# Attention and two MLPs on one core: MLP 2's second product of token blocks 0 and 1 by seven half-size products, in an order set by hand

## The chip, the cores and the metric

The kernel runs on one core of one Trainium2 chip. The metric is the device time of one execution in microseconds (us), taken as the median of several runs; less is better. TensorE (PE) multiplies matrices into PSUM, VectorE (DVE) and ScalarE (ACT) read PSUM and SBUF, GpSimd (POOL) works in SBUF, and SyncE (SP) issues the DMAs.

## The reference

Inputs are float32 (B = 4, H = 8, S = 576, D = 64; 2304 tokens of width 512):

```
kv  = einsum('bhsd,bhse->bhde', k, v)
o   = einsum('bhsd,bhde->bhse', q, kv)
o   = o / sqrt(mean(o*o, -1) + 1e-6) * g_norm
x   = o reshaped to [2304, 512]
x   = relu(x @ w_in)**2 @ w_out                  # MLP 1, hidden width 2048
p   = probs / (probs.sum(-1) + 1e-9)             # [2304, 4]
out = sum over e of p[:, e] * (relu(x @ w1[e]) @ w2[e])   # MLP 2, hidden width 4 x 1024
```

## The kernel before

**Tiling.** The tokens are cut into five blocks: 0 to 3 of 512 tokens, and 4 of 256. The hidden width of each MLP is cut into slices of 256: eight for MLP 1 (v = 0 to 7) and sixteen for MLP 2. MLP 2 goes through its sixteen slices twice: v = 8 to 23 for blocks 0, 1 and 4 (the first group), v = 24 to 39 for blocks 2 and 3 (the second group). Each float32 operand is split into a high part `hi` and a remainder `lo` (`split`, L224: an ACT copy and a POOL subtraction), and a product is three matmuls: lo x hi, hi x lo, hi x hi.

**Units.** The program is a list of units, each a function call that issues the instructions of a small step. f: the first product of one block (24 matmuls per slice, with 512 columns, or 256 for block 4). s: the first product of a pair of blocks, by seven half-size products in Winograd's form (`g1s`, seven units of six matmuls). h: the second product of one block in plain form (`g2b`, L834: six matmuls for 128 tokens, whose result is weighted by p and added into the block's accumulator on DVE, L852). q: the second product of a pair by seven half-size products (`g2q`, L774: fourteen units of three matmuls, output transposed, each added into an accumulator on DVE, L797). Before the change q serves the second group alone; the first group uses h for all its blocks.

**What q needs.** For q the hidden values are already multiplied by p (`hidden_t`, L726, four DVE instructions per slice, from a copy of p spread over the partitions), and the right-hand operands are four quarters b11, b22, b21 and four sums t1 to t4 of the hidden tile `hb` (`second_right`, L741, units r: r0 to r6 split an operand, r7 to r10 form t1 to t4). q's left-hand side needs the weight b and the weight sums bs. For h the hidden tile is split instead by an ACT relu and a DVE instruction (L829, L830).

**Weights.** In the first group each slice's weights are loaded (raw), summed and split (units w: `operands`, `left_sums`, `second_sums`), and the split parts a, a2, b and bs are stored to DRAM; the second group fetches them from there (`fetch`). The sums for a and a2 are made on DVE (tile w), those for bs on POOL (tile ws).

**Order.** `rest()` writes the unit list of MLP 1 and MLP 2, with stretches around the turns set by hand (`TURNS`, `END`). Through the first group the compiler's planner places the instructions on the compute engines and only SP keeps the written order; from v = 25 all engines keep it. At the turn the operands of blocks 2 and 3 are made from their accumulators (units x, `right`); these accumulators stay in SBUF through the first group.

**Buffers.** PSUM has eight banks (pool ps). `tmp` has eight buffers of 2 KB per partition. In the second group `hb` alternates between two tiles.

## Time and profile before

| what | value |
|---|---|
| median of three runs | 1198.81 us (1198.78 to 1198.99) |
| the profiled execution's own time | 1202.84 us |
| its span, from the first to the last instruction | 1201.0 us |
| mean granted TensorE clock | 0.998 |
| busy: PE, DVE, POOL, ACT | 1174.3, 849.4, 709.5, 442.3 us |
| moved by DMA | 186.18 MB |

Busy time is the union of an engine's instructions. PE's matmuls overlap in the record, so that the distance between two starts, not the duration of one, is the price of a matmul. A wait is idle time of an engine ahead of an instruction, with what released it.

### The profile page before, as it was taken

What the parts mean: (1) busy time and instruction counts of PE and PEld (TensorE: products, weight loads), DVE (VectorE), ACT (ScalarE), POOL (GpSimd) and SP (SyncE); (2) the same over time, 40 slices, a digit from 0 to 9 for tenths busy, and PEclk for the clock granted to TensorE, in tenths of its full rate; (3) what the DMA queues carried; (4) which work ended last, traced back from release to release, by engine and by line L of the source; (5) the groups of instructions that cost most, each with busy time, mean ns of one, the idle gap of its engine ahead of it and who ended that gap; (6) DMA issues with size and microseconds to landing.
All of it is one profiled execution on the core that took longest, in us unless ns stands there. A gap on an engine that the chain in (4) does not pass through costs nothing.

```text
span 1201.0 us, 15349 instructions
## 1 busy us (share of the span) xinstructions
PE 1174.3 (98%) x5642; PEld 982.7 (82%) x5642; DVE 849.4 (71%) x1268; ACT 442.3 (37%) x825; POOL 709.5 (59%) x588
## 2 busy tenths in 40 slices
...
GB/s 294 236 68 36 71 18 35 53 19 71 40 43 62 36 141 93 233 217 181 221 213 175 191 232 191 200 226 274 166 288 133 222 191 260 158 256 190 205 193 70
DMA packets 49392, 186.18 MB, mean 155 GB/s; under 512 B 5122, under 2 KB 13314, under 8 KB 37030
## 3 DMA queue, kind: packets, MB, share of 16 engines
...
q8 instruction: 45, 0.74, 0.2%
...
q10 hardware_dynamic: 288, 0.04, 0.0%
...
## 4 chain that ended last, share of the span: by engine, by line
PE 87%; DVE 5%; POOL 4%; issue 2%; ACT 1%; DMA 0%; POOLq 0%; DVEq 0%; ACTq 0%
PE p L842 18%; PE p L554 14%; PE p L540 13%; PE pc L679 8%; PE pa L679 8%; PE pd L679 8%; PE pb L679 4%; PE qc L784 3%; PE qd L784 3%; PE qa L784 3%; PE qb L784 2%; POOL hl L226 1%; PE pk L443 1%; PE po L458 1%; DVE u L261 1%
## 5 line engine op out<-in xcount | busy, mean ns | idle before, releaser
L842 PE MATMUL p<-b,hh 128*128 128x512 f32 x640 | 207.8, 390 | 0.5 <-ACT hh L829 0.5
L554 PE MATMUL p<-hh,b 128*128 128x512 f32 (+1 forms) x640 | 191.1, 371 | 0.0
L226 POOL TENSOR_TENSOR hl<-r,hh 128x512 fp32r<-128x512 f32 (+1 forms) x80 | 104.7, 1316 | 77.6 <-ACT hh L225 73.6
L540 PE MATMUL p<-x,a 128*128 128x512 f32 (+1 forms) x720 | 148.8, 362 | 0.2 <-POOL x L226 0.2
L842 PEld LDWEIGHTS p<-b,hh 128*128 128x128 f32 x640 | 120.3, 188 | 25.1 <-ACT hh L829 0.7
L540 PEld LDWEIGHTS p<-x,a 128*128 128x128 f32 x720 | 122.8, 189 | 22.1 <-POOL x L226 0.7
L554 PEld LDWEIGHTS p<-hh,b 128*128 128x128 f32 x640 | 117.6, 189 | 20.7 <-ACT hh L225 0.3
L561 DVE TENSOR_TENSOR acc<-p,acc 128x512 f32<-128x512 f32 (+1 forms) x140 | 86.1, 631 | 61.1 <-PE p L554 60.7
L852 DVE SCALAR_TENSOR_TENSOR acc<-p,p_sb,acc 128x512 f32<-128x512 f32 x150 | 108.8, 745 | 26.1 <-PE p L842 26.0
L842 PE MATMUL p<-b,hl 128*128 128x512 f32 x320 | 125.0, 391 | 0.2 <-DVE hl L830 0.2
L554 PE MATMUL p<-hl,b 128*128 128x512 f32 (+1 forms) x320 | 118.9, 372 | 3.4 <-POOL hl L226 3.4
L679 PE MATMUL pd<-o,a 128*128 128x512 f32 x384 | 98.0, 390 | 1.2 <-DVE pb L699 1.2
L679 PE MATMUL pa<-o,a 128*128 128x512 f32 x384 | 97.8, 390 | 0.0
L679 PE MATMUL pc<-o,a 128*128 128x512 f32 x384 | 97.7, 390 | 0.0
L679 PEld LDWEIGHTS pd<-o,a 128*128 128x128 f32 x384 | 71.9, 188 | 17.1 <-DVE pb L699 2.3
L226 POOL TENSOR_TENSOR a<-w,a 128x512 fp32r<-128x512 f32 x42 | 55.8, 1345 | 50.1 <-ACT a L225 50.1
L679 PEld LDWEIGHTS pc<-o,a 128*128 128x128 f32 x384 | 71.9, 188 | 15.4 <-DVE u L694 0.6
L679 PEld LDWEIGHTS pa<-o,a 128*128 128x128 f32 x384 | 72.0, 188 | 15.2 <-ACT p L690 0.3
L226 POOL TENSOR_TENSOR a<-raw,a 128x512 fp32r<-128x512 f32 x32 | 42.7, 1334 | 56.2 <-ACT a L225 56.2
L226 POOL TENSOR_TENSOR b<-raw,b 128x512 fp32r<-128x512 f32 x32 | 40.7, 1293 | 56.5 <-ACT b L225 56.5
L554 PEld LDWEIGHTS p<-hl,b 128*128 128x128 f32 x320 | 60.6, 189 | 15.5 <-POOL hl L226 5.6
L842 PEld LDWEIGHTS p<-b,hl 128*128 128x128 f32 x320 | 60.2, 188 | 11.8 <-DVE hl L830 0.5
(183 smaller groups left out, 2353.1 us busy)
## 6 DMA issues: line engine op xcount, KB each, us to landing
raw<-in_w SPq DMA_DIRECT2D x65, 512.0 KB, 4.2
a_kept<-a SPq DMA_DIRECT2D x32, 1024.0 KB, 8.5
a<-a_kept SPq DMA_DIRECT2D x32, 1024.0 KB, 10.4
b_kept<-b SPq DMA_DIRECT2D x16, 1024.0 KB, 6.7
bs_kept<-o SPq DMA_DIRECT2D x16, 1024.0 KB, 9.7
bs<-bs_kept SPq DMA_DIRECT2D x16, 1024.0 KB, 7.6
...
kvm<-in_kvm SPq DMA_DIRECT2D x10, 512.0 KB, 3.7
```

The costliest lines, as they stand in the source:

```text
L226: nc.gpsimd.tensor_tensor(out=lo, in0=full, in1=hi.bitcast(F32), op=ALU.subtract)
L261: nc.vector.scalar_tensor_tensor(out=u.bitcast(F32), in0=k, scalar=1.125 * 2.0**-15, in1=u.bitcast(F32), op0=ALU.is_ge, op1=ALU.mult,)
L443: nc.tensor.matmul(pk[:, :P], m[:, 0, n, :], m[:, 1, n, :], start=(n == 0), stop=False)
L458: nc.tensor.matmul(po[done : done + n, c * P : (c + 1) * P], q[:, c, done : done + n], kvd[(b * NPAIR + c) % NKVD], start=True, stop=True,)
L540: nc.tensor.matmul(pt[:, :n], w, x, start=(i == 0), stop=(i == len(steps) - 1))
L554: nc.tensor.matmul(pt[:, :n], w, h, start=(i == 0), stop=(i == len(steps) - 1))
L561: nc.vector.tensor_tensor(out=a, in0=pt[:, :n], in1=a, op=ALU.add)
L679: nc.tensor.matmul(pr[bank], x, y, start=(m == 0 and not more), stop=(m == len(steps) - 1), skip_group_check=more,)
L784: nc.tensor.matmul(pt, x, y, start=(m == 0 and not more), stop=(m == len(steps) - 1), skip_group_check=more)
L842: nc.tensor.matmul(pt, h, w, start=(i == 0), stop=(i == len(steps) - 1))
L852: nc.vector.scalar_tensor_tensor(out=a, in0=pt, scalar=pe, in1=a, op0=ALU.mult, op1=ALU.add)
```

## The change

In the first group the second product of blocks 0 and 1 is made by q units too; block 4 keeps h. So the transposed output holds blocks 0 to 3, and the first group's slices get the whole machinery of q: hidden values weighted by p, seven operand splits and four sums per slice. The sums t3 and t4 go to DVE in both groups. The splits of b and bs (`split_dma`) become two ACT copies (hi, and minus hi) and an accumulating DMA from POOL's queue that adds the full value. To make room, blocks 2 and 3 are stored to DRAM at the start of MLP 2 (units d10 and d11) and read back at the turn (d12 to d14); `hb` becomes a single tile in the space of block 2; p's spread copy is loaded anew every four slices (unit E, which is d7); tiles move between pools, and `tmp` has seven buffers. The loads, stores and weight steps become units of their own (d: `move`, u: `prepare`), and from x0.11 on all engines keep the written order: `FIRST` for v = 8, `STEPS` for v = 9 to 21, `TURN` for 22 to 24, `LATER` for 25 to 38 and `END`. In these lists S is the next s unit, q the next q unit of the slice before, p, v, n the previous, this and the next slice. The end of MLP 1 has a new order as well (`CHANGE`, not shown), in which x0 is cut into twelve units, with the sums of block pairs made in place.

```diff
-N2 = 2 * 512
-T2 = BLK[2][0] // P
+N2 = 4 * 512
+T4 = N2 // P
...
-    if v < NS1:
-        return [f"g{v}.{j}.{c}" for j in blk[::-1] for c in range(KD)]
-    if v >= V2:
-        return [f"q{v}.{n}" for n in (*range(6), 7, 6, *range(8, 14))]
-    return [f"h{v}.{j}.{t}" for j in blk[::-1] for t in range(BLK[j][1] // P)]
+    return [f"g{v}.{j}.{c}" for j in blk[::-1] for c in range(KD)]
...
+FIRST = """
+x0.11 s8.0.0 d8.7 d8.10 u8.7 s8.0.1 u8.8 s8.0.2 r8.0 s8.0.3 d9.0 u9.0 s8.0.4 s8.0.5 u8.9 r8.9 d8.5 u9.1 r8.5
+r8.7 r8.8 f8.4.0 d8.11 s8.0.6 d9.2 d9.7 d8.4 d8.6 r8.3 f8.4.1
+""".split()
+
+STEPS = """
+S q u{v}.3 q S r{p}.1 r{p}.4 h{p}.4.0 u{v}.5 r{p}.10 u{v}.4 S r{p}.2 q S u{v}.2 d{v}.4 q r{p}.6 d{n}.0 q
+u{v}.7 h{p}.4.1 q q S u{v}.8 d{n}.2 r{v}.0 S q q r{v}.9 r{v}.7 q S q u{v}.9 r{v}.3 q E q d{v}.6 u{n}.0 u{n}.1
+r{v}.5 f{v}.4.0 d{v}.5 q f{v}.4.1 r{v}.8
+""".split()
+
+TURN = """
+s22.0.0 q21.0 u22.3 r21.2 q21.1 h21.4.0 r21.1 r21.4 u22.4 q21.2 s22.0.1 s22.0.2 u22.5 r21.10 u22.2 s22.0.3
...
+LATER = """
+S d{v}.9 r{p}.1 d{n}.8 r{p}.4 r{p}.10 q r{p}.2 q S q S S q q r{p}.6 q S q q q r{v}.0 r{v}.7 q q r{v}.3 S q q
+r{v}.9 S q r{v}.8 r{v}.5
+""".split()
+
...
 END = """
...
+r38.4 s39.2.0 r38.10 q38.0 q38.7 q38.1 s39.2.1 s39.2.2 d39.9 s39.2.3 q38.10 q38.2 q38.8 s39.2.4 r38.2 r38.1
+r39.0 s39.2.5 r39.7 r38.6 r39.8 q38.6 s39.2.6 r39.4 r39.10 r39.9 q38.9 q38.12 q38.5 q38.4 q38.3 q39.0 r39.3
+q38.13 r39.5 q38.11 q39.7 r39.1 q39.2 r39.2 r39.6 q39.9 q39.1 q39.3 q39.8 q39.10 q39.5 q39.11 q39.12 q39.6
+q39.4 q39.13
+""".split()
...
+def second_stage():
+    r = list(FIRST)
+    for v in range(NS1 + 1, NV - 1):
+        if v == V2 - 2:
+            r += TURN
+        if V2 - 2 <= v <= V2:
+            continue
+        i, q = 0, iter([f"q{v - 1}.{n}" for n in (*range(6), 7, 6, *range(8, 14))])
+        for u in STEPS if v < V2 else LATER:
+            if u == "S":
+                r.append(f"s{v}.{GRP2[v >= V2][0][0]}.{i}")
+                i += 1
+            elif u == "q":
+                r.append(next(q))
+            elif u == "E":
+                r += [f"d{v + 1}.7"] * ((v + 1 - NS1) % (F2 // FS) == 0)
+            else:
+                r.append(u.format(v=v, p=v - 1, n=v + 1))
+    return r + END
...
-    tmp = ctx.enter_context(tc.tile_pool(name="tmp", bufs=8))
+    tmp = ctx.enter_context(tc.tile_pool(name="tmp", bufs=7))
...
-    def split(hi, lo, full):
+    def split(hi, lo, full, engine=nc.gpsimd):
         nc.scalar.activation(out=hi, in_=full, func=AF.Copy)
-        nc.gpsimd.tensor_tensor(out=lo, in0=full, in1=hi.bitcast(F32), op=ALU.subtract)
+        engine.tensor_tensor(out=lo, in0=full, in1=hi.bitcast(F32), op=ALU.subtract)
+
+    def split_dma(hi, lo, full):
+        nc.scalar.activation(out=hi, in_=full, func=AF.Copy)
+        nc.scalar.activation(out=lo, in_=hi.bitcast(F32), func=AF.Copy, scale=-1.0)
+        nc.gpsimd.dma_start(out=lo.bitcast(F32), in_=full, accum_op=ALU.add)
...
+    def bs_tile(v):
+        if v % 2:
+            return ext.tile([P, 2, 2, 512], F32R, tag="b3", name=f"bs{v}")
+        if v >= V2:
+            return xp.tile([P, 2, 2, 512], F32R, tag="xt", name=f"bs{v}", bufs=1)
+        return spare[0]
+
+    def keep(v, tag, t):
+        w_kept[v, tag] = kept.tile(list(t.shape), F32, name=f"{tag}_kept{v}")
+        nc.sync.dma_start(out=w_kept[v, tag], in_=t.bitcast(F32))
+
+    def move(v, n):
+        s = slice_of(v) - NS1
+        if n in (0, 2):
+            raw[v, n] = rawp.tile([P, 2, HW], F32, tag="raw", name=f"raw{v}_{n}")
+            nc.sync.dma_start(out=raw[v, n], in_=w32[s, :, n : n + 2, :])
...
+        elif n == 4:
+            keep(v, "a", w_t[v][0])
+            keep(v, "a2", w_t[v][1])
+        elif n == 5:
+            keep(v, "b", w_t[v][2])
+        elif n == 6:
+            keep(v, "bs", w_t[v][3])
+        elif n == 7:
+            load_p(v)
...
+            bs = bs_tile(v)
+            w_t[v] += [b, bs]
...
+        elif n in (10, 11):
+            j = n - 8
+            x_kept[j] = kept.tile([P, KD, 512], F32, name=f"x_kept{j}")
+            nc.sync.dma_start(out=x_kept[j], in_=acc_t[j])
+        elif n == 12:
+            t = xp.tile([P, KD, 512], F32, tag="xt", name="xk3", bufs=1)
+            nc.sync.dma_start(out=t, in_=x_kept[3])
+            acc_t[3] = [t[:, :2], t[:, 2:]]
+        else:
+            t = rawp.tile([P, 2, HW], F32, tag="raw", name=f"xk2_{n}")
+            nc.sync.dma_start(out=t, in_=x_kept[2][:, (n - 13) * 2 : (n - 12) * 2, :])
+            acc_t[2] = [t, None] if n == 13 else [acc_t[2][0], t]
+
+    def prepare(v, n):
+        if n == 0:
+            r = raw[v, 0].rearrange("p c (k f) -> p (c k) f", k=2)
+            w_t[v] = [wp.tile([P, 2, KD, FS], F32R, tag=tag, name=f"{tag}{v}") for tag in ("a", "a2")]
+            w_full[v] = left_full(v, r[:, 0:2], r[:, 2:4])
+        elif n in (1, 2):
+            r = raw[v, 0].rearrange("p c (k f) -> p (c k) f", k=2)
+            a = w_t[v][n - 1].rearrange("p x k (h f) -> p x (k h) f", h=2)
+            split(a[:, 0, 0:4, :], a[:, 1, 0:4, :], r[:, :, (n - 1) * P : n * P])
+        elif n in (3, 4):
+            left_split(v, n - 3, w_full[v][n - 3])
+        elif n == 5:
+            b = wp.tile([P, 2, FC, DM], F32R, tag="b", name=f"b{v}")
+            w_t[v].append(b)
+            split_dma(b[:, 0], b[:, 1], raw[v, 2])
+        elif n in (7, 8):
+            r = raw[v, 2]
+            if n == 7:
+                w_sums[v] = ext.tile([P, 2, HW], F32, tag="ws", name=f"ws{v}")
+            t = w_sums[v]
+            a11, a21, a12, a22 = (r[:, f, h * FS : (h + 1) * FS] for f in range(2) for h in range(2))
+            s2, s3, s4, s1 = (t[:, f, h * FS : (h + 1) * FS] for f in range(2) for h in range(2))
+            if n == 7:
+                nc.gpsimd.tensor_tensor(out=s1, in0=a21, in1=a22, op=ALU.add)
+                nc.gpsimd.tensor_tensor(out=s3, in0=a11, in1=a21, op=ALU.subtract)
+                return
+            nc.gpsimd.tensor_tensor(out=s2, in0=s1, in1=a11, op=ALU.subtract)
+            nc.gpsimd.tensor_tensor(out=s4, in0=a12, in1=s2, op=ALU.subtract)
+        else:
+            bs = bs_tile(v)
+            w_t[v].append(bs)
+            split_dma(bs[:, 0], bs[:, 1], w_sums.pop(v))
+
+    w_full, w_sums, x_kept = {}, {}, {}
...
+    def load_p(v, e=None):
+        t0 = pair_of(v)[0] * 4
+        if e is None:
+            e = (slice_of(v) - NS1) * FS // F2
+            if v == NS1:
+                t = p_t[v] = ext.tile([P, 2, 2, 512], F32, tag="a3", name="pb8")[:, 0]
+            elif v == V2:
+                t = p_t[v] = hp.tile([P, 2, 512], F32, tag="hl", name=f"pb{v}")
+            else:
+                if "u" not in p_t:
+                    p_t["u"] = accp.tile([P, 2, 2, 512], F32, tag="acc3", name="pu")
+                t = p_t["u"][:, 0]
+        else:
+            t = spare[0][:, e % 2].bitcast(F32)
...
+        if i == 7:
+            nc.vector.tensor_tensor(out=b11, in0=b12, in1=b11, op=ALU.subtract)
+        elif i == 8:
+            t2 = t_tmp["x"] = [tmp.tile([P, 512], F32, tag="tmp", name=f"t2_{g}_{k}") for k in range(2)]
+            for k in range(2):
+                nc.vector.tensor_tensor(out=t2[k], in0=b22[:, k], in1=b11[:, k], op=ALU.subtract)
+        elif i == 9:
+            nc.vector.tensor_tensor(out=b12, in0=b22, in1=b12, op=ALU.subtract)
+        elif i == 10:
+            t2 = t_tmp.pop("x")
+            for k in range(2):
+                nc.vector.tensor_tensor(out=b21[:, k], in0=b21[:, k], in1=t2[k], op=ALU.subtract)
...
+        if not full_t:
+            full_t.append(accp.tile([P, 4, 512], F32, tag="acc2", name="hb"))
+        pb = p_t[v] if v in p_t else p_t["u"][:, 0] if v < V2 else spare[0][:, e % 2].bitcast(F32)
...
-            engine = nc.vector if v in (V2, NV - 1) else nc.gpsimd
+            engine = nc.vector if v in (NS1, V2, NV - 1) or name in SUMS else nc.gpsimd
...
+    SUMS = ("t3", "t4")
...
-        adds = {"p6": (c12, c21), "p7": (c22,)}.get(p, ())
-        for c in adds:
-            nc.gpsimd.tensor_tensor(out=c, in0=c, in1=u2, op=ALU.add)
-        if p == "p7":
+        adds = {"p6": (c12, c21), "p7": (c22,)} if g else {"p6": (c22, c12, c21)}
+        for c in adds.get(p, ()):
+            engine = nc.gpsimd if g or c is not c22 else nc.vector
+            engine.tensor_tensor(out=c, in0=c, in1=u2, op=ALU.add)
...
-        if v >= V2:
+        if v >= NS1 and j in pair_of(v):
...
-    m = order.index("s25.2.0")
-    with tc.manual_schedule(engines={nc.sync.engine}):
-        for name in order[n:m]:
-            run(name)
     with tc.manual_schedule():
-        for name in order[m:]:
+        for name in second_stage():
```

## Rows read from the trace of the kernel before

**Rows 1.** The page's first part: busy us, share of the span, instructions.

```profile
PE 1174.3 (98%) x5642; PEld 982.7 (82%) x5642; DVE 849.4 (71%) x1268; ACT 442.3 (37%) x825; POOL 709.5 (59%) x588
```

**Rows 2.** Busy us of PE, PEld, DVE, ACT, POOL by stretch; clock, DMA share, GB/s.

```profile
40.00:240.00 200.00, 193.73 (x1007) 163.03 (x1006) 144.35 (x216) 103.27 (x194) 114.35 (x86) 0.99 0.20 64
...
464.00:490.00 26.00, 24.83 (x118) 20.07 (x117) 19.80 (x32) 10.81 (x21) 22.90 (x21) 1.00 0.52 206
...
567.41:593.45 26.04, 26.04 (x127) 22.02 (x126) 15.90 (x26) 8.14 (x15) 13.16 (x14) 1.00 0.56 203
...
912.00:1175.00 263.00, 263.00 (x1162) 217.86 (x1161) 206.76 (x315) 64.41 (x113) 191.96 (x152) 1.00 0.57 206
1175.00:1201.00 26.00, 16.57 (x65) 11.08 (x63) 17.74 (x28) 3.57 (x6) 15.95 (x12) 0.95 0.22 81
```

**Rows 3.** PE's waits, 463 to 890 us: total, times, longest.

```profile
PE p L842 <- ACT hh L829: 0.5, 1, 0.5
PE pd L679 <- DVE pb L699: 0.4, 1, 0.4
PE p L842 <- DVE hl L830: 0.2, 1, 0.2
```

**Rows 4.** PE in order of time: start, us, instructions; one slice.

```profile
567.41 1.52 PE L679 MATMUL pa<-o,a 128*128 128x512 f32 x6
568.77 1.52 PE L679 MATMUL pb<-o,a 128*128 128x512 f32 x6
...
579.65 1.60 PE L540 MATMUL p<-xb,a 128*128 128x256 f32 x12
581.09 0.40 PE L842 MATMUL p<-b,hh 128*128 128x512 f32 x1
...
593.45 1.52 PE L679 MATMUL pa<-o,a 128*128 128x512 f32 x6
```

**Rows 5.** DVE groups, whole run: count, busy us, mean ns, idle before.

```profile
L852 DVE SCALAR_TENSOR_TENSOR acc<-p,p_sb,acc 128x512 f32<-128x512 f32 x150 | 108.8, 745 | 26.1 <-PE p L842 26.0
...
L797 DVE TENSOR_TENSOR acct<-qa,acct 128x512 f32<-128x512 f32 x60 | 41.3, 688 | 12.1 <-PE qa L784 12.1
...
L830 DVE SCALAR_TENSOR_TENSOR hl<-p,hh 128x256 fp32r<-128x256 f32 x32 | 13.5, 422 | 10.8 <-ACT hh L829 10.8
```

**Rows 6.** Tile w, the weight sums on DVE: min/median/max ns.

```profile
L399 DVE TENSOR_TENSOR w<-raw x16: 415/426/1128, 435.6 to 796.2; 128x256 f32<-128x256 f32 x16
...
L400 DVE TENSOR_TENSOR w<-w,raw x16: 412/877/958, 436.3 to 797.5; 128x256 f32<-128x256 f32 x16
```

**Rows 7.** POOL and ACT groups, whole run.

```profile
L226 POOL TENSOR_TENSOR b<-hb,b 128x512 fp32r<-128x512 f32 x32 | 41.3, 1292 | 10.2 <-ACT b L225 10.2
...
L225 ACT ACTIVATE b<-hb 128x512 fp32r<-128x512 f32 x32 | 19.8, 620 | 2.5 <-DVE hb L736 2.5
```

**Rows 8.** Tile ws, the second weight sums on POOL.

```profile
L329 POOL TENSOR_TENSOR ws<-raw x16: 732/738/972, 470.8 to 821.9; 128x256 f32<-128x256 f32 x16
```

**Rows 9.** SP's queue in order of time, the same slice.

```profile
583.51 0.43 SPq L284 DMA_DIRECT2D b_kept<-b  x1
```

**Rows 10.** The list of DMA issues: count, KB each, median us to landing.

```profile
raw<-in_w SPq DMA_DIRECT2D x65, 512.0 KB, 4.2
a_kept<-a SPq DMA_DIRECT2D x32, 1024.0 KB, 8.5
a<-a_kept SPq DMA_DIRECT2D x32, 1024.0 KB, 10.4
...
o<-p_kept SPq DMA_DIRECT2D x4, 512.0 KB, 7.4
```

**Rows 11.** DVE groups at the turn, 853.8 to 882 us.

```profile
L616 DVE TENSOR_TENSOR t<-acc,t 128x512 f32<-128x512 f32 x4 | 5.8, 1446 | 0.0
L607 DVE TENSOR_TENSOR o<-t,o 128x512 fp32r<-128x512 f32 x4 | 4.3, 1087 | 0.2 <-ACT o L605 0.2
```

More of the change, by code (lines that the diff above doesn't have):

```diff
@@ L273, in split_w @@
         if len(parts) == 2:
-            left_sums(parts[0][0], *(full for _, full in parts))
+            for n, full in enumerate(left_full(parts[0][0], *(full for _, full in parts))):
+                left_split(parts[0][0], n, full)
             parts.clear()
@@ L402, in left_sums, with left_split @@
         nc.vector.tensor_tensor(out=s4, in0=a12, in1=s2, op=ALU.subtract)
-        for n in range(2):
-            a = w_t[v][n].rearrange("p x k (h f) -> p x (k h) f", h=2)
-            split(a[:, 0, 4:8, :], a[:, 1, 4:8, :], st[n].rearrange("p m k f -> p (m k) f"))
+        return [t.rearrange("p m k f -> p (m k) f") for t in st]
+    def left_split(v, n, full):
+        a = w_t[v][n].rearrange("p x k (h f) -> p x (k h) f", h=2)
+        split(a[:, 0, 4:8, :], a[:, 1, 4:8, :], full)
     def left(v, tile, x, op, k):
@@ L514, in fused_kernel @@
     h_t, acc_t = {}, {}
-    n_h = [0]
     def new_h(v, j):
-        pool, more = (ext, "3") if ext is not None and n_h[0] % 3 == 2 else (hp, "")
-        n_h[0] += 1
-        h_t[v, j] = [
-            pool.tile([P, FC, 512], F32R, tag=t + more, name=f"{t}{v}_{j}") for t in ("hh", "hl")
-        ]
+        h_t[v, j] = [hp.tile([P, FC, 512], F32R, tag=t, name=f"{t}{v}_{j}") for t in ("hh", "hl")]
         return h_t[v, j]
@@ L529, in g1 @@
         if fc == 0:
-            new_h(s, j)
+            if s < NS1:
+                new_h(s, j)
+            else:
+                pool, tag = (ext, "ws") if s == V2 - 1 else (hp, "hl")
+                t = pool.tile([P, 2, FC, n], F32R, tag=tag, name=f"h{s}_{j}")
+                h_t[s, j] = [t[:, 0], t[:, 1]]
         pt = ps.tile([P, 512], F32, tag="ps", name=f"p1_{s}_{j}_{fc}")
@@ L590, in right @@
             return
-        o = xp.tile([P, 2, 4, 512], F32R, tag="xs", name=f"o{g}_{i}", bufs=4)
-        if len(OPS[i]) == 1:
+        (b11, b21), (b12, b22) = (
+            acc_t[j] if isinstance(acc_t[j], list) else (acc_t[j][:, :2], acc_t[j][:, 2:]) for j in pair
+        )
+        if i == 7:
[10 more added lines that the diff above has]
+                nc.vector.tensor_tensor(out=b21[:, k], in0=b21[:, k], in1=t2[k], op=ALU.subtract)
@@ L593, in right @@
+        if i > 6:
+            return
+        n, m = divmod(i, 2)
+        name = OPS[n][m]
+        if m == 0:
+            o_new[n] = xp.tile([P, 2, 4, 512], F32R, tag="xs", name=f"o{g}_{n}", bufs=4)
+        o = o_new[n]
+        if name == "t4":
             spare[0] = o[:, :, 2:4, :]
             if g:
-                load_p(0)
-                load_p(1)
-        for m, name in enumerate(OPS[i]):
-            o_t[pair[0], name] = (o, m * 2)
-            for k in range(2):
-                hi, lo = o[:, 0, m * 2 + k, :], o[:, 1, m * 2 + k, :]
-                if name[0] == "b":
-                    split(hi, lo, x_part(pair, name, k))
-                    continue
-                full = t_sum(pair, name, k)
-                nc.scalar.activation(out=hi, in_=full, func=AF.Copy)
-                engine = nc.gpsimd if k else nc.vector
-                engine.tensor_tensor(out=lo, in0=full, in1=hi.bitcast(F32), op=ALU.subtract)
@@ L609, in t_sum @@
[L609 to L632 removed]
+                load_p(V2, 0)
@@ L636, in right_first @@
+                load_p(V2, 1)
+        o_t[pair[0], name] = (o, m * 2)
+        engine = nc.gpsimd if name in ON_POOL else nc.vector
+        hi, lo = (o[:, x, m * 2 : m * 2 + 2, :] for x in range(2))
+        if name == "t2":
+            for k in range(2):
+                split(hi[:, k], lo[:, k], t_tmp["x"][k], engine)
+        else:
+            split(hi, lo, dict(b11=b11, t1=b11, b21=b21, t4=b21, b22=b22, t3=b12)[name], engine)
+    o_new = {}
     def right_first(i):
```

273 lines of the change are left out of this document (84 added, 189 removed).

## The prediction

> **What bounds the kernel now.** I began with busy time by engine [rows 1]: TensorE (PE) is busy 98% of the span, every other engine 71% or less. A busy share can hide slow or idle matmuls, so I next cut the span into stages [rows 2]. In one slice of MLP 2's first group (567.41 to 593.45) PE is busy for all 26.04 us, at a granted clock of 1.00 (the 2.4 GHz level), while VectorE (DVE) has 15.9 us of work, GpSimd (POOL) 13.2 and the DMA engines a share of 0.56. PE's waits over that whole group come to 1.1 us [rows 3], so its length is its matmuls. In the second group (912 to 1175) PE is never idle either; DVE has 206.8 of 263 us and POOL 192.0.
>
> The price of a matmul is read from the start times in PE's timeline [rows 4], not from durations, since matmuls overlap. Six with 512 columns take 568.77 - 567.41 = 1.36 us, 0.2267 us each; twelve with 256 columns take 581.09 - 579.65 = 1.44 us, 0.12 each. A slice holds 42 (seven products) + 48 (h of blocks 0 and 1) + 12 (h of block 4) = 102 of the first kind and 24 of the second: 23.12 + 2.88 = 26.0 us, the slice seen [rows 4]. The model closes, so matmuls can be priced by count.
>
> **What the change removes from PE.** Per slice the 48 matmuls of the pair's second product become 14 units of 3 = 42. Six fewer are 1.36 us, a slice becomes 24.64 us, and 16 slices save **21.8 us**. The second group's matmuls are as before. This holds while everything else keeps under PE.
>
> **DVE per slice.** One second-group slice is 84 matmuls = 19.04 us of PE, so its window holds 13.8 slices and DVE has 206.8 / 13.8 = 15.0 us in each [rows 2]: 14 additions of q, 5 of the first product, 4 masked products. A slice of the first group now has these, plus t3 and t4 (2 x 0.69, by the addition of the same width [rows 5]), the four weight sums (3 x 0.43 + 0.88, by their medians [rows 6]), block 4's two hidden pieces and two accumulations (2 x 0.42 + 2 x 0.745) [rows 5]: 20.9 of 24.64 us, 85%. In the second group t3 and t4 move to DVE: 16.4 of 19.04, 86%. Full, but below PE.
>
> **POOL and ACT per slice.** POOL: seven operand splits, two sums (t1, t2), four splits of a and a2, 13 x 1.29 [rows 7], and four weight sums of 0.74 [rows 8]: 19.7 of 24.64 us, 80%. In the second group it falls by two sums, to 60%. The splits of b and bs leave POOL for two ACT copies and a DMA issued on POOL's queue that adds the full value in SBUF. ACT copies of 512 elements take 0.62 [rows 7]; with four of double width at up to 1.24 it has about 13 us, no limit. POOL's cost of issuing such a transfer is not in this trace: it lies between nothing and the 2.5 us each that would fill POOL's 5 us of slack. The operation nearest in kind is a store's issue on SP, 0.43 us [rows 9]; I take that, and the slack covers it.
>
> **The accumulating transfer** has no row either. It moves 512 KB and also reads its destination. From below it is a 512 KB load, 4.2 us; from above, by bytes moved, a 1 MB store, 8.5 us [rows 10]. b is not needed until the next slice, many us later. bs is the tight one: u9 stands after 7 first-product units (S), 2 h and 11 q of its step, which is 9.5 + 2.7 + 7.5 = 19.7 us; its first reader is the second q of the next step, at 24.64 + 1.36 + 0.68 = 26.7. That leaves 7 us behind PE's place in the order, and about 9.5 if ACT and POOL run a little ahead, as they can: bs's sums stand at 14.3 us, and only t1 (its hidden half ready near 16, done by 17.3) is ahead on POOL. I take the upper bound of 8.5 as just covered: cost 0. Behind it on SP is the store of bs, which PE does not wait for.
>
> **Single buffers and SP's order.** hb is one tile now where two alternated, so a hidden write waits for the splits of the slice before. The tightest is b22: its split r1 stands at 4.1 us of the step, the new write follows the sixth S at 15.6, 11 us behind; b21 has 12. POOL at 80% lags by less, so 0; a POOL later than that would hold DVE's queue, with the q additions in it, and then PE. On SP every d unit waits at the head of the queue: the stores of a and a2 (behind split u2) stand ahead of the next slice's load d0, placed at 10.2 us and wanted by u0 at 21.1; it lands in 4.2 [rows 10], so 6 us are left, and 0. DMA share: 0.56 of 26.04 us is 14.6 us for 5 MB, so 2 x 0.5 MB more, counted once or twice, make 17.5 to 20.4 of 24.64, at most 83%.
>
> **The start.** The hidden tile hb now lives in acc2, which holds MLP 1's block 2 until its 1 MB copy to DRAM (d8.10) has landed. Block 2's last g is followed only by g7.4 (24 x 0.12 = 2.9 us) and then s8.0.0 and s8.0.1 (2.7 us) before DVE wants to write hb. A store takes up to 8.5 us [rows 10]: DVE then stands 3 us late, and the additions queued behind it release the bank that the fifth product accumulates in. Against that, 1.2 us of idle at this place before [rows 2] may vanish. Bounds -1 and +4; I take **+1.5**.
>
> **New reloads of the probabilities** (E: slices 12, 16, 20). Each may go only after the seventh product's hidden write (about 20.4 us into the step), takes 7.4 us [rows 10], and is wanted at 28.7: just in time, from 0 to about 2 us each. I take **+0.5** in all.
>
> **The turn** (slices 22, 23, 24; PE 24.64 + 24.64 + 19.04 = 68.3 us). DVE has 3 x 15.0, eight t sums (5.5), one set of weight sums (2.2), block 4 (1.7 + 4.5), two closing additions (1.4), and x1's differences and lo parts. At the old turn four of eight differences took 1.446 us and the lo parts 1.087 [rows 11], against about 0.69; eight differences are then 8.5 us and six lo parts 6.5. Sum 75 us: 7 more than PE has. The surplus can be put off in part into the slices behind, each with 2.6 us of slack. Bounds 0 and 7; I take **+4**. POOL's 25 operand steps, 7 weight splits, 8 weight sums, 4 double splits of x1 and 4 closing additions are 63 us, 92%.
>
> The Trainium skill, page "SBUF — State Buffer" (section Who interferes with whom), says that a DVE instruction with two SBUF inputs contends with a GpSimd instruction that reads SBUF. This trace agrees where both are loaded: the 1.446 us differences [rows 11] and the 0.88 us weight sum beside one of 0.43 [rows 6]. Applied to every such instruction, the rule makes rival 1, below, 1187 to 1195; with the mix of these rows the sum is mine.
>
> **The end, and the rest.** In the last 26 us PE is busy for 16.6 [rows 2], and two chains of three closing additions on POOL (3 x 1.29 us each [rows 7]) stand in it. The new END brings all p5, p6 and p7 ahead of the last products, so the last chain goes earlier: between 0 and 3.9, I take **-1**. The tmp pool falls from 8 buffers to 7; that can only hurt where MLP 1 and the attention live on it. PE's idle time there is 6.3 us in 40 to 240 [rows 2], so I bound it by doubling, 0 to +6, and take 0, a choice: nothing in these rows names a tmp buffer as what PE waits for. The spills and reloads of blocks 2 and 3 (4 MB) have no reader for many us, beyond the start and the turn.
>
> **Sum.** -21.8 + 1.5 + 0.5 + 4 - 1 = -16.8 us. The profiled execution ran 1202.84 us with a span of 1201.0; its changed span should be 1184. The median of the runs is 1198.81, 4 us below that execution, so the forecast is **1182.0 us**.
>
> **Rivals.**
> 1. *DVE becomes the bound* at the turn and in part elsewhere. If every DVE instruction with two SBUF inputs ran at the worst seen (t3 and t4 1.446, weight sums 0.96 [rows 6, 11]), a first-group slice would need 24.1 of 24.64, a second-group one 17.9 of 19.04, and the turn up to 8 us more. For it: POOL rises from 50% to 80%, so it is met more often. Against it: DVE still has 2 to 15% over in steady slices. Late queues would cost some 5 to 12 us more: 1187 to 1195.
> 2. *The accumulating transfer lands late.* It is one wait per slice: PE's second q waits for bs. Every us beyond the 9.5 costs 1 us x 15 slices; from 10.6 us on, the 16.8 is gone, and at 12 us the kernel takes 1182 + 37 = 1219. For it: the a and a2 stores (2 MB) travel in the same stretch, and 1 MB reloads take 10.4 [rows 10]. Against it: twice the bytes of a 4.2 us load are 8.5.
> 3. *Nothing lost*: start, turn and reloads hidden, end shorter: 1198.8 - 21.8 - 2 = 1175.
> 4. *POOL's issue is dear* (above 2.5 us each): POOL passes 24.64 and sets the slice; each 0.5 us more costs 1.0 per slice and 16 in all, so at 3 us each the kernel ends near 1198.
>
> The Trainium skill, page "DMA: Bandwidth & Descriptors" (section Anatomy of one DMA), fits a GpSimd-issued transfer as 2.0 us + bytes / 436 GB/s, an estimate of 3.2 us for 512 KB; by it rival 2 would not happen and the sum stays as it is. No row of this trace shows such a transfer.
>
> **How the numbers follow.** My forecast (1176 to 1187) has 0.63, rival 1 0.18, rival 3 0.05, rival 2 0.10, rival 4 0.04. About 0.2% (2.4 us) is what a measurement here can tell from no change. Faster: 0.63 + 0.18 + 0.05 = 0.86; slower: 0.10 + 0.01; same: 0.03. The range takes my forecast's cases, rival 1 and the terms' lower bounds: 1175 to 1195.
>
> **What would show it.** PE start to start 24.6 us per slice in the first group, with PE waits under 0.3 us each; the second group's slices unchanged at 19.04; a PE wait on DVE near the first hidden writes (hb behind the store of block 2) and one of some us between slices 22 and 24; DVE 83 to 88% and POOL 78 to 90% in steady slices; the accumulating transfers landing within 9 us. A regular PE wait for bs at the second q of every step, or POOL above 97%, would make it wrong.

## The result, and the profile after

The changed kernel runs in 1187.36 us (median of four, 1185.91 to 1189.08), the kernel before in 1198.9 beside it: a ratio of 0.9898 [0.9878, 0.9917]. That is 11.5 us less, not the 16.8 of the sum. The profiled execution took 1188.53 us with a span of 1186.7, against 1202.84 and 1201.0. One of the runs below (after_tail) had a profile in a slowed execution, so of that kernel only times are told.

The page's first part, which answers to [rows 1]: PE is still busy for nearly the whole span; DVE and POOL have come up.

```profile
PE 1152.6 (97%) x5546; PEld 965.7 (81%) x5546; DVE 947.5 (80%) x1414; ACT 498.7 (42%) x871; POOL 795.9 (67%) x662
```

Busy time by stretch (columns as in [rows 2]): a steady slice of the first group, the turn, the second group.

```profile
560.00:585.00 25.00, 25.00 (x123) 21.18 (x122) 21.23 (x35) 11.56 (x18) 21.27 (x21) 1.00 0.81 258
850.00:875.00 25.00, 20.06 (x82) 14.71 (x81) 24.06 (x33) 8.59 (x13) 21.46 (x15) 1.00 0.93 326
900.00:1160.00 260.00, 259.89 (x1147) 214.87 (x1146) 221.10 (x341) 61.85 (x109) 156.26 (x123) 1.00 0.57 207
```

PE in order of time in the steady part, the same unit (block 4's h) in two successive slices:

```profile
560.68 1.52 PE L885 MATMUL p<-b,h 128*128 128x512 f32 x6
...
585.35 1.52 PE L885 MATMUL p<-b,h 128*128 128x512 f32 x6
```

585.35 - 560.68 = 24.67 us for a slice, forecast 24.64. In that stretch PE is busy for 25.00 of 25 us, DVE for 21.23 (85%, forecast 85%), POOL for 21.27 (85%; the sum had 80%, and its own list of signs 78 to 90%); the DMA share is 0.81 (bound 0.83). Between 480 and 845 us PE has no wait in the list. In the second group PE is busy for 259.89 of 260, DVE 85%, POOL 60%. The steady state came out as worked out; the loss lies at the seams, which are the start of slice 8, the turn and the end.

PE's waits from 463 to 890 us, where [rows 3] had 1.1 us:

```profile
PE pa L711 <- DMA a<-a_kept: 3.0, 1, 3.0
PE qb L830 <- ACT t L233: 2.1, 1, 2.1
PE pa L711 <- ACT p L722: 1.7, 2, 1.0
PE qb L830 <- POOL t L234: 1.1, 1, 1.1
PE pd L711 <- DVE pb L731: 0.9, 1, 0.9
PE pc L711 <- DVE u L726: 0.8, 1, 0.8
PE pa L711 <- POOL o L234: 0.4, 1, 0.4
PE qd L830 <- POOL t4b L234: 0.3, 1, 0.3
```

Of these 10.3 us, 2.4 stand in slice 8 (0.69 of the waits for p, and those for pc and pd), 7.9 at the turn, between 851 and 881 us. The 1.1 us of [rows 3] are slice 8's alone; the old turn had one wait, shown first, and the two longest of the new one follow:

```profile
896.33 0.74 PE L784 MATMUL qc<-t,bs 128*128 128x512 f32 x2 [1.12 <-POOL t L226]
```

```profile
860.03 0.49 PE L830 MATMUL qb<-t,bs 128*128 128x512 f32 x1 [2.13 <-ACT t L233]
878.22 1.66 PE L711 MATMUL pa<-o,a 128*128 128x512 f32 x6 [2.98 <-DMA a<-a_kept]
```

The whole turn, from slice 22's first matmul to slice 25's first (columns as above):

```profile
801.91:878.22 76.31, 68.39 (x316) 55.19 (x314) 69.97 (x99) 30.84 (x45) 65.06 (x51) 1.00 0.83 280
```

PE has the 68.4 us of matmuls that were forecast (68.3) and 7.9 of waits. DVE is busy for 70.0 us of the 76.3, where the prediction's sum had 75, and POOL for 65.1 (forecast 63).

The turn in detail, POOL, then ACT, then DVE in order of time; the bracket is the idle time ahead of a group and what ended it:

```profile
851.06 2.37 POOL L234 TENSOR_TENSOR o<-xk,o 128x1024 fp32r<-128x1024 f32 x1 [0.84 <-ACT o L233]
...
854.65 1.74 POOL L234 TENSOR_TENSOR t<-t3f,t 128x512 fp32r<-128x512 f32 x1
856.34 1.75 POOL L234 TENSOR_TENSOR b<-hb,b 128x512 fp32r<-128x512 f32 x1
858.04 1.27 POOL L786 TENSOR_TENSOR t2f<-hb,t1f 128x512 f32<-128x512 f32 x1
860.05 1.47 POOL L234 TENSOR_TENSOR t<-t2f,t 128x512 fp32r<-128x512 f32 x1 [0.74 <-ACT t L233]
```

```profile
849.90 1.06 ACT L233 ACTIVATE o<-xk 128x1024 fp32r<-128x1024 f32 x1 [1.23 <-DMA xk<-x_kept]
...
859.34 0.63 ACT L233 ACTIVATE t<-t2f 128x512 fp32r<-128x512 f32 x1 [5.39 <-POOL t2f L786]
```

```profile
853.61 3.33 DVE L644 TENSOR_TENSOR xk<-xk,t 128x512 f32<-128x512 f32 x2
```

PE's product qb at 860.03 needs t2, and t2 is the last of POOL's row: an operand of x1 at double width (2.37), three splits, then the sum t2f, done at 859.31; ACT, idle for 5.39 us, copies it and POOL splits it. Two of POOL's splits take 1.74 and 1.75 us instead of 1.28 while DVE makes x1's in-place differences (3.33 for two). SP's queue in the same stretch:

```profile
864.54 3.23 SPq L844 DMA_DIRECT2D out<-acct  x3
867.86 2.19 SPq L319 DMA_DIRECT2D a<-a_kept  x2
```

The fetch of a for slice 25 stands behind three output stores. They hold SP's queue for 3.23 us, most of it waiting for the results that they store (each issue takes 0.33 to 0.96 us), and PE meets the fetch late by 2.98 us.

The end, POOL, DVE and then SP's queue:

```profile
1171.54 1.30 POOL L851 TENSOR_TENSOR acct<-acct,acct 128x512 f32<-128x512 f32 x1
1172.80 2.53 POOL L851 TENSOR_TENSOR acct_r<-acct_r,acct 128x512 f32<-128x512 f32 x2
1175.27 1.27 POOL L851 TENSOR_TENSOR acct<-acct,acct 128x512 f32<-128x512 f32 x1
1176.49 2.49 POOL L851 TENSOR_TENSOR acct_r<-acct_r,acct 128x512 f32<-128x512 f32 x2
```

```profile
1176.57 0.69 DVE L838 TENSOR_TENSOR acct<-qc,acct 128x512 f32<-128x512 f32 x1 [2.40 <-POOL acct L851]
```

```profile
1175.35 4.00 SPq L844 DMA_DIRECT2D out<-acct_r  x2
1179.44 1.37 SPq L844 DMA_DIRECT2D out<-acct  x3
```

PE's last group:

```profile
1174.06 0.84 PE L830 MATMUL qd<-t4b,b 128*128 128x512 f32 x3
```

It ends at 1174.06 + 0.84 = 1174.90, 11.8 us before the span's end; before, it ended at 1194.57 with 6.4 us behind it. POOL goes from splits straight into six closing additions, 1171.54 to 1178.98, and DVE stands 2.40 us for one of them. SP's queue waits too: its second store, of POOL's last sum, can go only at 1179.01, and the other six of the eight stand behind it, the last issued at 1182.19. Of the 5.4 us more behind PE, some 2.7 are the later last addition (4.1 us behind PE's end, before 1.4) and some 2 the seven stores left to issue after it, where before there were four.

### The profile page after: what moved, and what is told of

Its sections match the earlier page's. It is cut to its first block, busy times and chain, and to the rows that moved or that the text cites. A ratio compares the mean times of both kernels' runs of the same rounds, so it can differ in the third digit from the quotient of the medians.

```text
span 1186.7 us, 15541 instructions
## 1 busy us (share of the span) xinstructions
PE 1152.6 (97%) x5546; PEld 965.7 (81%) x5546; DVE 947.5 (80%) x1414; ACT 498.7 (42%) x871; POOL 795.9 (67%) x662
## 4 chain that ended last, share of the span: by engine, by line
PE 86%; DVE 5%; DMA 3%; POOL 2%; issue 2%; ACT 1%; SPq 0%; POOLq 0%; DVEq 0%; ACTq 0%
PE p L578 15%; PE p L564 13%; PE pa L711 8%; PE pc L711 8%; PE pd L711 8%; PE qc L830 7%; PE qa L830 7%; PE qd L830 7%; PE pb L711 4%; PE qb L830 3%; PE p L885 3%; PE po L483 1%; PE pk L468 1%; DMA b_kept<-b 1%; DMA a<-a_kept 1%
## 5 line engine op out<-in xcount | busy, mean ns | idle before, releaser
L234 POOL TENSOR_TENSOR b<-hb,b 128x512 fp32r<-128x512 f32 x64 | 85.1, 1331 | 71.7 <-ACT b L233 68.5
L233 ACT ACTIVATE b<-hb 128x512 fp32r<-128x512 f32 x64 | 40.1, 628 | 168.8 <-PE qa L830 162.8
L234 POOL TENSOR_TENSOR a<-w,a 128x512 fp32r<-128x512 f32 x42 | 59.9, 1428 | 73.0 <-ACT a L233 73.0
L711 PEld LDWEIGHTS pd<-o,a 128*128 128x128 f32 x384 | 71.9, 188 | 16.5 <-DVE pb L731 1.6
L838 DVE TENSOR_TENSOR acct<-qc,acct 128x512 f32<-128x512 f32 x90 | 61.7, 686 | 4.3 <-POOL acct L851 4.3
L838 DVE TENSOR_TENSOR acct<-qa,acct 128x512 f32<-128x512 f32 x90 | 61.4, 684 | 0.1
L234 POOL TENSOR_TENSOR t<-t3f,t 128x512 fp32r<-128x512 f32 x32 | 43.4, 1356 | 21.3 <-ACT t L233 21.3
L830 PE MATMUL qd<-t4b,b 128*128 128x512 f32 x192 | 54.5, 391 | 0.6 <-POOL t4b L234 0.3
L830 PE MATMUL qa<-b,b 128*128 128x512 f32 x192 | 53.8, 389 | 0.0
```

The lines of the kernel that those rows point to most:

```text
L233: nc.scalar.activation(out=hi, in_=full, func=AF.Copy)
L234: engine.tensor_tensor(out=lo, in0=full, in1=hi.bitcast(F32), op=ALU.subtract)
L711: nc.tensor.matmul(pr[bank], x, y, start=(m == 0 and not more), stop=(m == len(steps) - 1), skip_group_check=more,)
L830: nc.tensor.matmul(pt, x, y, start=(m == 0 and not more), stop=(m == len(steps) - 1), skip_group_check=more)
L838: nc.vector.tensor_tensor(out=to, in0=pt, in1=to, op=ALU.add)
```

## The experiments

The changes are to the kernel before (labels that begin with before) or to the changed kernel.

**before_42: PE's count alone.**

```diff
     steps = [(h[:, f, ts], b[:, w, f, :]) for f in range(FC) for h, w in ((hh, 1), (hl, 0), (hh, 0))]
+    if j < 2 and i4 == 3:
+        steps = steps[:3]
```

> The kernel before with 6 of the 48 matmuls of each first-group slice's pair left out (the second half of the hidden width in the last 128 tokens of blocks 0 and 1, so those tokens lack it), nothing else. Theory (TensorE's matmul count sets the first group): 16 x 6 x 0.2267 = 21.8 us less, ratio 0.982, slices of 24.64 us without PE waits. Rival (part of the gain is lost to the other engines even without the new work): under 18 us.

Measured: 1177.78 us, 0.9803 [0.9788, 0.9818], 24.3 us below the median before of the same session. In the profiles the stretch from slice 8's first matmul to the last matmul fell from 730.8 to 708.97 us, by 21.83; what the two spans have more (1201.0 against 1177.3) lies ahead of it, where nothing was changed. A price by count, with nothing else touched, holds to 0.1 us in 21.8.

**before_tmp7: seven tmp buffers in the kernel before** (`bufs=8` to `bufs=7`).

> The kernel before with 7 tmp buffers in place of 8. The profile after reaches MLP 2 3.2 us earlier than the profile before. Theory: that is not the change's doing but the execution that was profiled, so this kernel runs within 0.2% of before. Rival: the pool's size or the planner's answer to it moves the first half by 3 us either way, ratio 0.9975 or 1.0025.

Measured: 1199.93 us, 0.999 [0.998, 0.9999]: at most 0.2% less, no loss, and the term of nothing stands for the time. Within it the waits moved: in this profile PE waits 3.1 us at the end of MLP 1 (1.0 before) and not at all at the start of slice 8 (1.2 before).

**after_pool_split: the accumulating transfer replaced by the POOL subtraction of the kernel before.**

```diff
 def split_dma(hi, lo, full):
     nc.scalar.activation(out=hi, in_=full, func=AF.Copy)
-    nc.scalar.activation(out=lo, in_=hi.bitcast(F32), func=AF.Copy, scale=-1.0)
-    nc.gpsimd.dma_start(out=lo.bitcast(F32), in_=full, accum_op=ALU.add)
+    nc.gpsimd.tensor_tensor(out=lo, in0=full, in1=hi.bitcast(F32), op=ALU.subtract)
```

> The changed kernel with b and bs split on POOL (one ACT copy and one POOL subtraction of 1024 columns each) in place of the accumulating DMA. POOL gains 2 x 2.5 us per slice and loses 2 x 0.88 of issue: 20.9 + 3.3 = 24.2 of 24.64 us. Theory (POOL's queue then runs late and PE waits): 10 to 40 us slower than the changed kernel, ratio to before 0.998 to 1.023, PE waits on POOL in every slice. Rival (POOL just fits): within 5 us of the changed kernel, ratio 0.988 to 0.994.

Measured: 1207.12 us, 1.005 [1.0033, 1.0067]. The same steady stretch (columns as above) and PE's longest group of waits in 560 to 900 us:

```profile
560.00:585.00 25.00, 24.69 (x119) 20.31 (x118) 24.05 (x33) 9.44 (x16) 24.86 (x19) 1.00 0.60 225
```

```profile
PE p L884 <- DVE h L872: 4.6, 10, 1.7
```

POOL is full (24.86 of 25), and DVE rises from 21.23 to 24.05 us with the same instructions. PE now waits in nearly every slice for DVE's h, and the change would have lost time. In this order the transfer is what makes it pay.

**after_sums_pool: t3 and t4 back on POOL** (`SUMS = ("t3", "t4")` to `SUMS = ()`).

> The changed kernel with t3 and t4 formed on POOL again in all slices but the first, v = 24 and the last. DVE falls by 1.5 us per slice, POOL rises by 2.6, to 23.5 of 24.64. Theory (at the turn both DVE and POOL are full, so work moved between them does not help): steady slices still 24.7, the turn 2 to 6 us longer, ratio to before 0.991 to 0.996. Rival (the turn waits for DVE alone): 3 us shorter, ratio 0.987.

Measured: 1196.84 us, 0.9957 [0.9945, 0.9969], 9.5 us more than the changed kernel. The steady slices still hold (POOL 24.55 of 25, PE 25.00), but PE has two waits of 1.86 and 6.04 us for DVE that it hadn't, at 751.60 and 830.83. What stood ahead of the long one, DVE, POOL, then PE:

```profile
819.03 10.75 DVE L424 TENSOR_TENSOR w<-raw 128x256 f32<-128x256 f32 x1
```

```profile
827.97 1.51 POOL L234 TENSOR_TENSOR t<-t2f,t 128x512 fp32r<-128x512 f32 x1
```

```profile
830.83 2.93 PE L564 MATMUL p<-xb,a 128*128 128x256 f32 x12 [6.04 <-DVE acc L895]
```

One of DVE's weight sums, which takes 0.43 us [rows 6], lasts 10.75 us, from 819.03 to 829.78. POOL works without a pause from 819.29 to 829.48, and the sum ends 0.3 us after it stops. The accumulation that PE waits for stands behind that sum in DVE's queue. So the cost of a POOL without slack came through DVE.

**after_turn_dma: two DMA units of the turn earlier.**

```diff
-s23.0.4 ... q22.13 s24.2.1 d23.4 q23.1 ... d24.9 q23.2 q23.3 ... s24.2.4 d25.8 q23.6
+s23.0.4 d23.4 ... q22.13 s24.2.1 q23.1 ... d24.9 d25.8 q23.2 q23.3 ... s24.2.4 q23.6
```

> The changed kernel with two transfers moved in the order of the turn: the store of a and a2 of slice 23 (d23.4) to behind the fifth product of slice 23, some 15 us earlier, and the fetch of a and a2 of slice 25 (d25.8) to behind d24.9, ahead of the output stores. Theory (PE's 2.98 us wait at the start of slice 25 is that fetch, which stands on SP's queue behind output stores and late kept stores): the wait goes, 2.5 to 3.5 us less than the changed kernel. Rival (the DMA engines are full at the turn, share 0.93, so the fetch lands late wherever it stands): under 1 us.

Measured: 1192.8 us, 0.9939 [0.992, 0.9958]: neither's number. The wait for slice 25's a is gone, as the order theory said, but the stores of a and a2 (1 MB each, issued at 828.9 and 836.0) now run beside the accumulating transfer of b, issued at 832.4. PE's wait for it, and the landing of that one transfer:

```profile
843.56 4.68 PE L885 MATMUL p<-b,h 128*128 128x512 f32 x12 [5.21 <-DMA b<-raw]
```

```profile
DMA to landing us min/median/max: 11.1/11.1/11.1
```

It landed 11.1 us after its issue, where the transfers of b take 5.3 in the changed kernel. This is rival 2, brought about by moving a store.

**after_turn_dve: three quarters of DVE's in-place differences of x1 left out** (128 of 512 columns are made; one of three such edits is shown).

```diff
+            n = 128 if g else 512
-            nc.vector.tensor_tensor(out=b11, in0=b12, in1=b11, op=ALU.subtract)
+            nc.vector.tensor_tensor(out=b11[:, :, :n], in0=b12[:, :, :n], in1=b11[:, :, :n], op=ALU.subtract)
```

> The changed kernel with x1's in-place differences (t1, t3, t4 of blocks 2 and 3) made over 128 of 512 columns, so those operands are left unfinished: DVE loses some 4.3 us at the turn, nothing else changes. Theory (DVE's surplus at the turn is what PE's waits of 4.9 us there come from): 3 to 4.5 us less. Rival (the waits come from POOL's and ACT's chains and transfers, DVE only queues beside them): under 1.5 us.

Measured: 1187.83 us, 0.9886 [0.9862, 0.9911], no different from the changed kernel; the turn's waits are 6.96 us instead of 7.91, and 0.96 of them is a new one, for the accumulating transfer of b. POOL at the turn, then two of the shortened differences, then the stretch around them:

```profile
854.28 1.34 POOL L234 TENSOR_TENSOR t<-t3f,t 128x512 fp32r<-128x512 f32 x1
855.58 1.34 POOL L234 TENSOR_TENSOR b<-hb,b 128x512 fp32r<-128x512 f32 x1
```

```profile
853.11 2.65 DVE L647 TENSOR_TENSOR xk<-xk,t 128x128 f32<-128x128 f32 x2
```

```profile
850.00:875.00 25.00, 21.49 (x83) 15.98 (x81) 22.84 (x32) 8.23 (x13) 20.27 (x15) 0.93 0.93 330
```

The edit took less of DVE's time away than expected. The two differences beside POOL's splits still take 2.65 us (3.33 in the changed kernel) with a quarter of their columns, and all that were shortened fell from 6.0 to 3.8 us, by 2.3 instead of 4.3. What it gave came through POOL: the splits beside them take 1.34 us (1.74 in the changed kernel), and PE's wait for t falls from 2.13 to 1.39. The time shows none of it, with the granted clock at 0.93 in this stretch (1.00 in the changed kernel). The run is thus a weak test of a DVE surplus. The stretch of the whole turn shown above is the better one: DVE's work there is only 1.6 us more than PE's.

**after_tail: the closing additions of one quarter on DVE.**

```diff
-            engine = nc.gpsimd if g or c is not c22 else nc.vector
+            engine = nc.gpsimd if c is not c22 else nc.vector
```

> The changed kernel with the closing additions of c22 in the second group on DVE in place of POOL. At the end POOL makes six additions of 1.26 us in a row and DVE's third last addition waits 2.4 us for them. Theory (the end is that POOL chain): 2 to 3 us less. Rival (the end is the output stores and their landing): under 0.7 us.

Measured: 1181.93 us, 0.9845 [0.9828, 0.9862], 5.4 us less than the changed kernel, more than was expected. The profiles of after_three and after_swap_tail, which hold the same edit, show the stretch behind the last matmul at 8.07 and 8.50 us instead of 11.80. So 3.3 to 3.7 us of it are shown there; in after_swap_tail the way from slice 8 to the last matmul is as long as in the changed kernel (714.3 us), and the rest isn't placed.

**after_start: another order of the first slice.**

```diff
-u8.7 s8.0.1 u8.8 s8.0.2 r8.0 s8.0.3 d9.0 u9.0 ... r8.7 r8.8 f8.4.0 d8.11 ... r8.3 f8.4.1
+u8.7 s8.0.2 s8.0.1 u8.8 r8.0 s8.0.3 f8.4.0 d9.0 u9.0 ... r8.7 r8.8 f8.4.1 d8.11 ... r8.3
```

> The changed kernel with slice 8's first product in another order: the product in bank b between the two that share bank a, block 4's first half between the two that share bank c, its second half ahead of the last product. Theory (PE's 2.4 us of waits at the start are additions into a bank that ACT or DVE still reads, not the store of block 2): 1.5 to 2.4 us less. Rival (hb waits for the store of block 2): no change within 0.5 us.

Measured: 1191.8 us, 0.9933 [0.9915, 0.9952]. The three waits at the start (2.41 us) shrink to 0.23 with the store of block 2 where it was: they were products waiting for ACT and DVE to read the banks of the products before, not hb waiting for the store. But the first slice's transfer into bs (tile o), issued at 468.6 together with the stores of a and a2 (468.6 and 469.3), landed 11.5 us later. In the changed kernel the same stores were issued 2.0 and 3.6 us behind it, and it landed in 5.5. PE in order of time, and the stretches around it:

```profile
480.24 1.62 PE L830 MATMUL qc<-t,o 128*128 128x512 f32 x3 [6.52 <-DMA o<-ws]
481.66 2.61 PE L711 MATMUL pa<-o,a 128*128 128x512 f32 x6
```

```profile
475.00:480.00 5.00, 0.00 (x0) 0.00 (x0) 0.00 (x0) 0.00 (x0) 1.40 (x2) 0.71 0.97 303
480.00:485.00 5.00, 4.76 (x13) 3.83 (x14) 0.64 (x1) 3.07 (x5) 1.91 (x2) 0.60 0.76 299
```

**after_three: the start of after_start with bs stored ahead of a (d8.6 before d8.4), slice 25's fetch earlier (d25.8 behind d24.9), and the closing additions of after_tail.**

> The changed kernel with three edits at three places. (1) Start: the order of slice 8 of after_start, and the store of bs (d8.6) ahead of the store of a and a2 (d8.4), so that SP waits for the accumulating transfer of bs before it issues 2 MB of stores. (2) Turn: the fetch d25.8 behind d24.9, while d23.4 stays where it was. (3) End: the closing additions of c22 on DVE. Theory (the accumulating transfer takes some 5.5 us alone and 11 us beside 2 MB of stores, and that alone made the two moved orders slower): no wait of PE on an accumulating transfer, 0.2 to 0.5 us of waits at the start, the slice-25 wait under 1.5 us, an end of 6 us from PE's last matmul; 7 to 10 us less than the changed kernel, ratio 0.981 to 0.984. Rival (it is the faster PE order itself that meets the transfer too early): PE still waits 2 to 6 us for it at the start, ratio 0.984 to 0.987.

Measured: 1180.87 us, 0.9846 [0.9827, 0.9865]. The fetch's wait is gone, and no new one came at the turn, since the stores stayed; at the start 2.49 us are left for the same transfer, landed after 7.4 us beside a load of p. The three edits together are not measurably better than after_tail alone.

**after_swap_tail: after_tail, with t2's sum ahead of a split at the turn** (r23.8 and r23.1 exchanged).

> The changed kernel with the c22 additions on DVE, and r23.8 (t2 formed on POOL) ahead of r23.1 (b22's split on POOL) in the turn. PE waits 2.13 + 1.05 us there for the split of t2, which stands behind t2's forming, and that behind b22's split of 1.75 us, whose result PE needs only one q later. Theory (POOL's order sets these waits): 1.5 to 1.8 us of the 3.2 go. Rival (t2's forming waits for DVE's hidden write or its contention): under 0.5 us goes.

Measured: 1181.54 us, 0.9841 [0.9827, 0.9855]. PE's waits for t2 become 1.18 and 2.29 us instead of 2.13 and 1.05: one less and one more. Sum and splits are POOL's work, whatever their order. Nothing was gained over after_tail.

**after_turn2: after_tail, slice 25's fetch earlier, and at the turn the sums for bs and the reading back of block 2 before x1.3.**

```diff
-x1.2 s23.0.4 q22.8 ... x1.3 s23.0.5 q22.9 u23.7 q22.10 u23.8 r23.9 x1.4 d23.14 r23.7
+x1.2 u23.7 u23.8 d23.14 s23.0.4 q22.8 ... x1.3 s23.0.5 q22.9 q22.10 r23.9 x1.4 r23.7
```

> The changed kernel with the c22 additions on DVE, d25.8 behind d24.9, and in the turn the sums of bs for slice 23 (u23.7, u23.8) and the reload of the last quarter of block 2 (d23.14) ahead of s23.0.4. POOL is idle for 2.8 us just there and full for 10 us when PE waits, and ACT waits 1.2 us for that reload. Theory (the turn's waits of 4.9 us ahead of slice 25 are POOL's queue behind a late reload): 2.5 to 4.5 us of them go, some 10 us less than the changed kernel, ratio 0.980 to 0.983. Rival (they are DVE's and ACT's chains, whatever POOL's order): under 1 us of them goes, ratio 0.983 to 0.986.

Measured: 1184.5 us, 0.9869 [0.9853, 0.9885], 2.6 above after_tail, with intervals that touch. PE at the turn:

```profile
851.16 0.50 PE L711 MATMUL pa<-o,a 128*128 128x512 f32 x1 [1.86 <-ACT p L722]
852.75 1.42 PE L711 MATMUL pa<-o,a 128*128 128x512 f32 x5 [1.09 <-POOL o L234]
```

The read-back of block 2, meant to come earlier, came 1.45 us later counted from slice 8's start (844.21 - 458.33 against 845.02 - 460.59): SP's queue waited ahead of it for the transfer of b and for the sums on POOL. ACT's copy of x1 still waits for it (2.15 us, 1.23 in the changed kernel), and POOL takes 3.02 us for the operand that took 2.37. The two waits for p and o grow from 1.41 to 2.95 us, and a wait of 1.20 us for the transfer of bs is new.

**after_all: after_turn2 with the start of after_three, in which slice 8's weight sums and their split now stand ahead of x0's last unit.**

> after_turn2 with the start of after_three and bs's sums and split for slice 8 (u8.7, u8.8, u8.9) ahead of block 4's operand, so that their accumulating transfer is issued some 5 us earlier. Theory (the start's wait of 2.5 us in after_three is this transfer's issue, behind POOL and ACT work that could stand later): under 0.5 us of waits between 460 and 480, 2 us less than after_turn2, ratio 0.978 to 0.981. Rival (POOL is full at the end of MLP 1, and the sums put there hold up its last splits): the same time moves to waits before slice 8, ratio equal to after_turn2 within 0.1%.

Measured: 1186.24 us, 0.9878 [0.9855, 0.9901]. The start keeps two waits of 1.27 us (the transfer was issued at 457.4 and is no longer one of them), the turn's waits are 7.0 us (7.4 in after_turn2). The best versions are thus after_three, after_swap_tail and after_tail, near 1181 us, below both kernels and not told apart.

## Why the prediction was right, point by point

The direction and the main term held, and the time lies within the range, 5.4 us above the forecast. It is 0.4 us above the forecast's own case (1176 to 1187), in the stretch given to rival 1, though not by rival 1's mechanism, as told below. One term, the end, lay outside its bounds; the start and the reloads came out lower and made up for a part of it. Between the two profiled executions, from the start of slice 8 to the last matmul, 730.8 us became 714.3: 16.5 less. PE's waits in it account for the 5.3 that lack to 21.8: the turn 7.9 against 1.1, slice 8's start 2.4 against 1.2, the last slices 0.25 against 2.9, together 5.4. The stretch behind the last matmul is 5.4 longer. Ahead of slice 8, MLP 1 is 1.45 us shorter (376.54 to 375.09 from the last matmul of attention to slice 8); attention itself, whose code the change leaves as it is, ended between 81.6 and 87.2 us in eight profiles of both versions. With it (1.7 less in this pair) -16.5 + 5.4 - 1.45 - 1.7 makes the 14.3 us between the two spans; the medians lie 11.5 apart. The prediction's terms with their measured sizes, below, make -21.8 - 0.2 + 0 + 6.8 + 2.7 = -12.5, where it had -16.8.

- *PE's count* (-21.8): exact, by before_42 and by the slices' 24.67.
- *DVE per slice and in the second group* (85 and 86%): 85 and 85% measured, and no wait.
- *POOL per slice* (80%): 85%. The sum of 80% (13 x 1.29 + 4 x 0.74 = 19.7) left the issues of the accumulating transfer to the slack. Each, taken as 0.43 us, was mis-sized:

```profile
L239 POOL DMA_DIRECT2D b<-raw x16: 836/849/1007, 420.3 to 834.7; - x16
...
DMA to landing us min/median/max: 4.5/5.2/6.8
```

It costs 0.84 to 1.01 us, twice the choice and well inside the bounds (the lines for bs, left out, lie between); with two a slice the sum is 21.5 us, 87%. Rival 4, which needed more than 2.5 us, did not occur. after_pool_split shows the edge it stood for: POOL at 24.86 of 25.
- *The accumulating transfer* (cost 0, landing within 4.2 to 8.5): right in the changed kernel, where it lands in 4.5 to 6.8. The margin is thin: o<-ws was issued at 568.61 and first read at 577.19, 8.6 us later; at the turn it is used up, where bs was issued at 849.33, landed 5.5 us later and was read at 854.88. Rival 2 stays outside only as long as the stores of a and a2 keep their places: with one of them issued 2.4 us ahead (579.23 against 581.66) a transfer of b still took 5.2 us, while the two orders that moved the pair met 11.1 and 11.5 us.
- *The start* (+1.5): -0.2 in all, by another mechanism. Slice 8 has 2.4 us of waits against 1.2, not through the store of block 2, as after_start shows, but through banks read late: +1.2, near the choice by luck. The idle time of [rows 2] that was to vanish is in this 1.2 and did not; what vanished is 1.45 ahead of it, in MLP 1, which was in no term. The 8.5 us taken as the most that a store needs is a median: the two stores here landed after 4.9 and 9.9.
- *Reloads of p* (+0.5): no wait at slices 12, 16 or 20; 0.
- *The turn* (+4, bounds 0 to 7): +6.8, the largest mis-sized term but one, and its reason fell. It was worked out as a surplus of DVE work of 7 us over PE's 68.3. DVE is full for 25 us of it (24.06), but over the whole turn it worked 70.0 us, not 75, and was idle for 6.3. What PE meets is POOL's chain to t2 (3.2 us), ACT and POOL behind a late read-back (1.4), the fetch behind SP's stores (3.0), and 0.3 more for POOL. Both chains are read from what released each wait; no run here removed the first two. Contention with DVE is a part of POOL's: its two slow splits make 0.9 us. Rival 1, read as DVE setting the pace, is by these readings not what happened, though the time lies at its lower end.
- *The end* (-1, bounds 0 to -3.9): +2.7, outside its bounds and the term that failed most. The waits ahead of the last matmul did fall by 2.7. The step took for granted that the closing chains would move with it; they moved onto a POOL that was still splitting operands, and 5.4 us of additions, and of stores queued behind them, came out behind PE. after_tail gives 3.3 to 3.7 of them back by moving two additions.
- *Single hb buffer, SP's order, DMA share, tmp*: 0 each, as taken.

The Trainium skill, page "SBUF — State Buffer" (section Who interferes with whom), says that a DVE instruction with two SBUF inputs contends with a GpSimd instruction that reads SBUF. The runs agree from both sides: POOL's split beside DVE's differences 1.74 us, 1.34 with these cut; DVE 24.05 us for what took 21.23 once POOL was full. The prediction applied the rule to DVE's time alone; at the turn it was POOL's that mattered. And its rival 1 took the worst times seen before, 0.96 us for a weight sum, as the worst there are: in after_sums_pool one lasted 10.75, until POOL paused.

What stays open: whether the turn can be had below 7 us by moving x1's splits off POOL, which no run tried; and where the 2 us of after_tail lie that are not behind the last matmul.
